# Batch 0 of a linear-attention and MLP kernel: q turned by 64x64 products, q.kv with 64 rows per product, and a new planned order

## The chip, the cores and the metric

The kernel runs on one core of one Trainium2 chip. The metric is the device time of one execution in microseconds; the time of before is the median of 3 runs. Rows of the profile use these names: PE is TensorE's matrix products, PEld its weight loads, DVE is VectorE, ACT is ScalarE, POOL is GpSimd, SP is SyncE, which issues most of the DMAs. "L789" is line 789 of the kernel.

## The reference

For 8 batches of 8 heads, with 576 rows of 64 numbers in each of q, k and v:

```
kv  = einsum('bhsd,bhse->bhde', k, v)            # 64x64 per head
out = einsum('bhsd,bhde->bhse', q, kv)           # 576x64 per head
out = out / sqrt(mean(out*out, -1) + 1e-6) * g_norm
x   = heads side by side: (8, 576, 512)
a1  = alpha1 * x + beta1
u   = x + lam * einsum('ts,bsd->btd', w_tok, a1)  # mixes the 576 rows
a2  = alpha2 * u + beta2
y   = u + lam * (max(a2 @ w_ch1, 0) @ w_ch2)      # 512 -> 2048 -> 512
```

## The kernel before, in words

The program is a list of operations, each with an engine, an assumed cost in microseconds, what it reads and what it writes. A list scheduler (`schedule`, L180) plays the engines forward with these costs and so fixes the order of each engine's queue and the PSUM banks; `synchronize` then puts in the waits. At run time every engine works its queue strictly in that fixed order. `plan` (L123) runs the scheduler several times, sets priorities from what it finds, and at last disturbs them at random with given seeds (`shake`, L164, here one seed, 15). It covers all operations that lie ahead of the first MLP products of batch 0. Wherever the model leaves PE without work before the first of those products, the scheduler puts a "warm" product of zeros (L1429, assumed 0.22 us) into PE's queue, so these are a fixed part of the program.

Per batch there are these stages:

- kv: k and v of a head multiplied into 64x64 (`kv_first`, L628, for batch 0; L691 and L701 for the others).
- q turned, so that the 64 columns of a head lie on partitions (`qt_first`, L649 and L663, for batch 0).
- q.kv (`qkv_groups`, L789 for batch 0; L782 and L401 for the others), and behind it the norm of each head: square (ACT, L819), sum (DVE, L821), root (ACT, L824), reciprocal (DVE, L827), multiplication into `xm`/`xtl` (DVE, L840), multiplication by alpha1, lam and g into `rt`/`rtt` (L844, DVE or POOL), multiplication by g (POOL, L848).
- token mixing with w_tok (`tok_first`, L972 for batch 0), an addition to x (L989), turning of the result (L1007) and a copy into `a2t` (L1016, L1017).
- MLP: `ch1` (L1056 with L401 for batch 0, L1075) into `ht`, and `ch2` (L1121), then the output.

w_tok itself is loaded (L1219, L1222) and turned once (L1260, L1278), and its row sums are made (L1301). w_ch1 comes in four chunks of 1 MB (L1340), each turned into bf16 by two copies (L1346); chunk i is needed by `ch1` groups 4i to 4i+3. All loads of this time go through SP in a fixed order.

Batch 0's attention is computed in fp32. Its first half (heads 0 to 3, called a=0) and second half (a=1) are loaded separately. In `qt_first`, one pair of heads takes 8 fp32 products: a stationary block of q of 128 rows (tokens) and 64 columns, and the 128x128 identity as the moving operand; the two heads of a pair fill the lower and the upper 64 partitions of one PSUM bank. A copy of 512 columns per pair (`act_dve`, L654) puts them into `qt32`. The last 64 tokens are turned in `tail` by PE's transpose operation (L663).

In q.kv of batch 0, one product takes 128 partitions of `qt32` (two heads, one above the other) and 128 tokens as the stationary operand, and a block-diagonal 128x128 `kv32` as the moving one: two 64x64 blocks of kv and two blocks of zeros, which a memset (L1229) writes. A group is two token blocks and four heads (4 products), the last group of a half is the 64 tokens at the end (2 products). So a half has three groups of 4, 4 and 2 products, and each has a norm of its own.

PE's records for fp32 products come in pairs: one product of L628, L649 or L789 leaves two records. A form such as "128*64 128x128 f32" means a stationary operand of 128 rows and 64 columns and a moving operand of 128 rows and 128 columns.

## Time and profile before

| | us |
|---|---|
| median of 3 runs | 368.47 (368.40 to 368.56) |
| the profiled execution, its own time | 368.05 |
| span in its trace | 366.2 |
| time around the span | 1.85 |
| first product of `ch1` of batch 0 on the chain | 38.63 after the span's start |
| L649 on the chain, both halves | 3.87 |
| L789 on the chain, all four pieces | 5.12 |
| warm products on the chain from 11.15 on | 3.88 |

The span is the time from the first to the last record of the traced execution. The chain of waits follows the last instruction back to whatever released each step; its pieces are given with start, length, engine and line, and "x32" is the number of records in the piece. The granted TensorE clock is 1.00 throughout.

### The profile page before, as it was taken

What the parts mean: (1) busy time and instruction counts of PE and PEld (TensorE: products, weight loads), DVE (VectorE), ACT (ScalarE), POOL (GpSimd) and SP (SyncE); (2) the same over time, 40 slices, a digit from 0 to 9 for tenths busy, and PEclk for the clock granted to TensorE, in tenths of its full rate; (3) what the DMA queues carried; (4) which work ended last, traced back from release to release, by engine and by line L of the source; (5) the groups of instructions that cost most, each with busy time, mean ns of one, the idle gap of its engine ahead of it and who ended that gap; (6) DMA issues with size and microseconds to landing.
All of it is one profiled execution on the core that took longest, in us unless ns stands there. A gap on an engine that the chain in (4) does not pass through costs nothing.

```text
span 366.2 us, 7069 instructions
## 1 busy us (share of the span) xinstructions
PE 360.6 (98%) x3164; PEld 205.8 (56%) x2876; DVE 198.4 (54%) x313; ACT 159.2 (43%) x268; POOL 81.7 (22%) x71
## 2 busy tenths in 40 slices
PE   7999999999999999999999999999999999999996
PEld 3787445467754554457654554457654554457644
DVE  4287699773973197735764176915933165720021
ACT  2464974237830298107650188107630186007600
POOL 4064602700450007100530006400620006200000
PEclk9999999999999999999999999999999999999999
DMA  8999999999777897439904499233404110420012
GB/s 257 319 290 319 384 382 273 265 250 249 211 141 158 246 259 178 101 94 309 230 18 115 138 304 177 50 110 85 90 7 108 59 30 0 59 100 30 0 57 88
DMA packets 92423, 59.87 MB, mean 163 GB/s; under 512 B 59549, under 2 KB 82341, under 8 KB 92264
## 3 DMA queue, kind: packets, MB, share of 16 engines
q1 hardware_dynamic: 92368, 59.41, 62.5%
q8 instruction: 24, 0.39, 0.5%
q14 instruction: 7, 0.06, 0.0%
q10 hardware_dynamic: 24, 0.01, 0.0%
HBM read 38.56 MB, written 9.44 MB: 131 GB/s over the span
## 4 chain that ended last, share of the span: by engine, by line
PE 97%; DMA 2%; SPq 0%; DVE 0%; issue 0%
PE ps L1121 34%; PE ps L1075 19%; PE ps L1056 16%; PE ps L920 8%; PE ps L691 4%; DMA qf<-in_q_dram 2%; PE ps L401 2%; PE ps L782 2%; PE ps L789 1%; PE ps L942 1%; PE ps L972 1%; PE ps L1007 1%; PE ps L1429 1%; PE ps L649 1%; PE ps L1102 1%; PE ps L701 1%
## 5 line engine op out<-in xcount | busy, mean ns | idle before, releaser
L1121 PE MATMUL ps<-w,ht 128*128 128x512 bf16 x560 | 126.0, 379 | 0.0
L848 POOL TENSOR_TENSOR xm<-xm,g_bc 128x512 f32<-128x512 f32 (+1 forms) x36 | 47.4, 1316 | 186.6 <-DVE rt L844 184.7
L1121 PEld LDWEIGHTS ps<-w,ht 128*128 128x128 bf16 x560 | 53.1, 98 | 63.0 <-issue 1.2
L1045 ACT ACTIVATE ht<-ps,hb 128x512 bf16<-128x512 f32 (+1 forms) x96 | 70.5, 739 | 40.5 <-PE ps L1075 32.8
L1075 PE MATMUL ps<-a2t,w 128*128 128x320 bf16 x512 | 71.9, 299 | 0.0
L1075 PEld LDWEIGHTS ps<-a2t,w 128*128 128x128 bf16 x512 | 49.3, 98 | 20.2 <-ACT ht L1045 0.3
L1056 PE MATMUL ps<-a2t,w 128*128 128x512 bf16 x256 | 59.7, 379 | 0.0
L1131 DVE TENSOR_TENSOR xm<-ps,xm 128x512 f32<-128x512 f32 x31 | 21.4, 689 | 50.4 <-PE ps L1121 50.3
L718 ACT ACTIVATE kvd<-ps 64x128 bf16<-64x128 f32 x28 | 7.6, 271 | 78.5 <-PE ps L701 78.1
L1056 PEld LDWEIGHTS ps<-a2t,w 128*128 128x128 bf16 x256 | 24.3, 97 | 29.6 <-issue 1.2
L821 DVE TENSOR_REDUCE small<-sq 128x16 f32<-128x1024 f32 (+2 forms) x20 | 20.5, 1028 | 22.9 <-ACT sq L819 22.9
L920 PE MATMUL ps<-rt,wt 128*128 128x512 bf16 x112 | 28.8, 379 | 0.0
L501 ACT ACTIVATE qs<-qf 128x1024 bf16<-128x1024 f32 (+1 forms) x15 | 14.2, 964 | 26.7 <-DMA qf<-in_q_dram 26.1
L927 DVE TENSOR_TENSOR xm<-ps,xm 128x1024 f32<-128x1024 f32 x14 | 17.1, 1222 | 14.5 <-PE ps L920 14.5
L1046 ACT ACTIVATE ht<-ps 128x512 bf16<-128x512 f32 (+1 forms) x32 | 20.6, 650 | 6.8 <-PE ps L1075 3.3
L819 ACT ACTIVATE sq<-ps 128x1024 f32<-128x1024 f32 (+2 forms) x20 | 17.4, 873 | 7.3 <-PE ps L789 4.3
L840 DVE TENSOR_TENSOR xm<-ps,small 128x1024 f32<-128x1024 f32 (+1 forms) x18 | 19.8, 1103 | 0.4
L723 DVE TENSOR_TENSOR kvd<-ps,kvd 64x128 bf16<-64x128 f32 x28 | 8.1, 288 | 20.5 <-ACT kvd L718 20.0
L844 DVE TENSOR_TENSOR rt<-xm,e1g_bc 128x1024 bf16<-128x1024 f32 (+1 forms) x17 | 19.0, 1125 | 0.1
L582 DVE TENSOR_TENSOR qs<-qf,qs 128x1024 bf16<-128x1024 f32 x12 | 15.3, 1284 | 6.8 <-ACT qs L501 6.8
L920 PEld LDWEIGHTS ps<-rt,wt 128*128 128x128 bf16 x112 | 10.9, 98 | 12.9 <-issue 0.4
L691 PEld LDWEIGHTS ps<-vf,kf 128*64 128x64 f32 x448 | 14.2, 138 | 5.0 <-issue 5.0
(119 smaller groups left out, 334.2 us busy)
## 6 DMA issues: line engine op xcount, KB each, us to landing
out_dram<-xm SPq DMA_DIRECT2D x31, 256.0 KB, 2.5
kf<-in_k_dram SPq DMA_DIRECT2D x7, 1024.0 KB, 10.3
vf<-in_v_dram SPq DMA_DIRECT2D x7, 1024.0 KB, 8.0
qf<-in_q_dram SPq DMA_DIRECT2D x7, 1024.0 KB, 8.0
stg<-in_moe_w_ch_dram SPq DMA_DIRECT2D x3, 1024.0 KB, 13.8
kf<-in_moe_w_ch_dram SPq DMA_DIRECT2D x2, 1024.0 KB, 14.6
kf<-in_k_dram SPq DMA_DIRECT2D x2, 576.0 KB, 5.2
vf<-in_v_dram SPq DMA_DIRECT2D x2, 576.0 KB, 6.3
```

Of the source, the lines that this page charges most:

```text
L691: m = e.matmul(out(h), kf[:, buf, h, c, :], vf[:, buf, h, c, :], start=(c == 0 and h < 4 * a + 2), stop=False, skip_group_check=True)
L821: P.op("DVE", dve_us(64 * m), lambda e: e.tensor_reduce(out=smv, in_=sqv.rearrange("p (h d) -> p h d", h=m), axis=AX.X, op=ALU.add), r=[(" ...
L840: P.op("DVE", dve_us(64 * m), lambda e: e.tensor_tensor(out=x3, in0=split(raw()), in1=inv, op=ALU.mult), r=[t, ("sm", sms)], w=xk, pri=-200)
L844: lambda e: e.tensor_tensor(out=r_, in0=x, in1=eb, op=ALU.mult),
L848: P.op("POOL", pool_us(64 * nh), lambda e, xc=xc: e.tensor_tensor(out=xc, in0=xc, in1=g_bc[rows, None, :].to_broadcast([nr, nh, DH]), op=A ...
L920: m = e.matmul(t.ap()[:, i, :], tok_w(b, sc, c), rsrc(b, sc), start=(sc == 0), stop=(sc == 4))
L1045: o = P.op("ACT", act_us(n) + 0.09, lambda e: e.activation(dst, src(), ACT.Relu, bias=hb[:, fj:fj + 1]) if b > 1 else e.activation(dst, sr ...
L1046: dst, src(), ACT.Relu, bias=hb[:, fj:fj + 1]) if b > 1 else e.activation(
L1056: m = e.matmul(t.flat(), w, a2t[:, dj, 0:512], start=(dj == 0), stop=(dj == 3))
L1075: m = e.matmul(t.ap()[:, i, 0:320], w1[:, dj, 128 * fj:128 * fj + 128], a2t[:, dj, 320 * i:320 * i + 320], start=(dj == 0), stop=(dj == 3))
L1121: m = e.matmul(t.flat(), ht[:, fj, 128 * c:128 * c + 128], w2[:, fj, :], start=(fj == 0), stop=(fj == 15))
L1131: P.op("DVE", dve_us(512), lambda e: e.tensor_tensor(out=x, in0=t.flat(), in1=x, op=ALU.add), r=[t] + keys, w=keys)
```

## The change

- `qt_first`: the two pairs of a half become one operation `main(a)` with 32 products. Each takes 64 rows (tokens) and 64 columns of one head as the stationary operand and a 64x64 corner of the identity as the moving one; the four products of a set lie in the four 64x64 quarters of the array: rows by token half `r`, output partitions by head `x`. The output goes to two banks, one for each token half, and two copies of 512 columns (two runs of 256) take it into `qt32`. The transposes of the last 64 tokens stay.
- `kv32` holds only the 64x64 blocks, one above the other; its memset goes, and the copies behind `kv_first` write columns 0 to 63.
- q.kv of batch 0: `first(hs)` replaces the three groups of a half. Its first operation has 16 products: 64 rows of `qt32` (one head) by 128 tokens as the stationary operand, 64 columns of `kv32` as the moving one. The lower head of each pair writes one bank, the upper head another, and they take turns. A second operation does the 64 tokens at the end with 4 products into two banks. Three norms follow: two of 512 columns (two heads, all four token blocks), one of 256 columns that reads two banks.
- The norm's code becomes a function of its own, `norm`, used by both kinds of groups. The keys that order readers and writers of x and rt are kept for 2 heads instead of 4. POOL's multiplication by g takes pieces of 256 columns as before in batch 0.
- The assumed costs: 1.12 for `main` (before 0.95 for each of two pairs), 1.0 and 0.2 for the two operations of `first` (before 0.28 for each token block, so 1.4 a half).
- `shake` uses other shares and widths, and the plan takes four seeds, (2, 103, 114, 147), in place of (15,).

```diff
@@ shake
-            return {o: pri[o] + (rnd.gauss(0.0, 2.0) if rnd.random() < 0.1 else 0.0)
+            share, by = (0.02, 0.1, 0.3)[seed % 3], (1.0, 3.0)[seed % 2]
+            return {o: pri[o] + (rnd.gauss(0.0, by) if rnd.random() < share else 0.0)
                     for o in movable}
@@ kv_first
-                        e, kv32[rows, 2 * a:2 * a + 2, 64 * h:64 * h + 64],
-                        t.ap(rows)[:, :, 0:64]), r=[t, "kvz"], w=[("kv32", a, h)])
+                        e, kv32[rows, 2 * a:2 * a + 2, 0:64], t.ap(rows)[:, :, 0:64]),
+                        r=[t], w=[("kv32", a, h)])
@@ qt_first
-            def pair(pr):
-                t = P.ptile(1)
+            def main(a):
+                t = P.ptile(2)
 
                 def f(e):
-                    for c in range(4):
-                        for h in range(2):
-                            m = e.matmul(t.flat(slice(64 * h, 64 * h + 64))[
-                                :, 128 * c:128 * c + 128], qf[:, 4 * (pr // 2) + 2 * h + pr % 2, c, :], ident[:],
-                                start=True, stop=True)
+                    for y in range(2):
+                        for c in range(4):
+                            for x, r in ((0, 0), (0, 1), (1, 0), (1, 1)):
+                                rows = slice(64 * r, 64 * r + 64)
+                                o = 256 * y + 64 * c
+                                m = e.matmul(t.ap(slice(64 * x, 64 * x + 64))[:, r, o:o + 64],
+                                             qf[rows, 4 * a + 2 * x + y, c, :],
+                                             ident[rows, rows], start=True, stop=True)
                     return m
-                P.op("PE", 0.95, f, r=["ident", ("qf", pr // 2)], w=[t])
-                P.op(act_dve(512), 0, lambda e: copy(e, qt32[:, pr, 0:512], t.flat()),
-                     r=[t], w=[("q32", pr)])
+                P.op("PE", 1.12, f, r=["ident", ("qf", a)], w=[t])
+                for y in range(2):
+                    P.op(act_dve(512), 0, lambda e, y=y: copy(
+                        e, qt32[:, 2 * a + y, 0:512].rearrange("p (c r s) -> p r c s", c=4, r=2),
+                        t.ap()[:, :, 256 * y:256 * y + 256].rearrange("p r (c s) -> p r c s", c=4)),
+                        r=[t], w=[("q32", 2 * a + y)])
@@ qkv_groups
+            def first(hs):
+                a = hs.start // 4
+                aa = [("kv32", a, i) for i in range(2)]
+                ts = [P.ptile(1) for i in range(2)]
+
+                def product(e, o, x, y, lo, n):
+                    r = slice(64 * x, 64 * x + 64)
+                    return e.matmul(o, qt32[r, 2 * a + y, lo:lo + n], kv32[r, 2 * a + y, 0:64],
+                                    start=True, stop=True)
+
+                def f(e):
+                    for c in range(4):
+                        for y in range(2):
+                            for x in range(2):
+                                o = 128 * c + 64 * y
+                                mm = product(e, ts[x].flat()[:, o:o + 64], x, y, 128 * c, 128)
+                    return mm
+                P.op("PE", 1.0, f, r=QT + KVD + aa + [("q32", 2 * a), ("q32", 2 * a + 1)], w=ts)
+                for x, t in enumerate(ts):
+                    h = hs.start + 2 * x
+                    norm(t, (0, 1, 2, 3), slice(h, h + 2))
+                last = P.ptile(2)
+                rows = rows_of(0, 4)
+
+                def g(e):
+                    for y in range(2):
+                        for x in range(2):
+                            mm = product(e, last.ap(rows)[:, x, 64 * y:64 * y + 64], x, y, 512, 64)
+                    return mm
+                P.op("PE", 0.2, g, r=QT + KVD + aa + [("q32t", a)], w=[last])
+                norm(last, (4,), hs)
...
-                def f32(e):
-                    a = h0 // 4
-                    for i, c in enumerate(cs):
-                        for j in range(2):
-                            mm = e.matmul(
-                                t.flat(rows)[:, 256 * i:256 * i + 256].rearrange(
-                                    "p (x y d) -> p y x d", x=2, y=2)[:, j],
-                                qt32[:, 2 * a + j, 128 * c:min(128 * c + 128, 576)],
-                                kv32[:, 2 * a + j, :].rearrange("p (x d) -> p x d", x=2),
-                                start=True, stop=True)
-                    return mm
-                if b == 0:
-                    P.op("PE", 0.28 * nc_, f32, r=QT + KVD + [("kv32", h0 // 4, i)
-                                                             for i in range(2)]
...
@@ memsets
-        P.op("DVE", 0.4, lambda e: e.memset(kv32, 0.0), w=["kvz"])
@@ plan
-        P.plan(due, 8, (15,))
+        P.plan(due, 8, (2, 103, 114, 147))
```

More of the change, by code (lines that the diff above doesn't have):

```diff
@@ L672, in qt_first @@
             for a in range(2):
-                yield lambda a=a: pair(2 * a)
-                yield lambda a=a: pair(2 * a + 1)
+                yield lambda a=a: main(a)
                 yield lambda a=a: tail(a)
@@ L754, in xkeys @@
             base = ("x", b % 2, c) if c < 4 else ("xt", (b // 2) % 2, b % 2)
-            return [base + (a,) for a in range(hs.start // 4, hs.stop // 4)]
+            return [base + (a,) for a in range(hs.start // 2, hs.stop // 2)]
         def rkeys(b, c, hs=ALL[0]):
             base = ("rt", b % 2, c) if c < 4 else ("rtt", b % 2)
-            return [base + (a,) for a in range(hs.start // 4, hs.stop // 4)]
+            return [base + (a,) for a in range(hs.start // 2, hs.stop // 2)]
         cnt = {"ch": 0}
         def qkv_groups(b):
+            def first(hs):
[26 more added lines that the diff above has]
+                norm(last, (4,), hs)
             def group(cs, hs):
@@ L768, in group @@
                 t = P.ptile((m + 7) // 8)
-                rows = rows_of(b, cs[0])
-                nr = rows.stop - rows.start
-                n = cnt["ch"]
-                cnt["ch"] += 1
-                sqs, sms = n % 2, n % 4
                 aa = range(hs.start // 4, hs.stop // 4)
@@ L784, in f, with norm @@
                     return mm
-                def f32(e):
-                    a = h0 // 4
-                    for i, c in enumerate(cs):
-                        for j in range(2):
-                            mm = e.matmul(
-                                t.flat(rows)[:, 256 * i:256 * i + 256].rearrange(
-                                    "p (x y d) -> p y x d", x=2, y=2)[:, j],
-                                qt32[:, 2 * a + j, 128 * c:min(128 * c + 128, 576)],
-                                kv32[:, 2 * a + j, :].rearrange("p (x d) -> p x d", x=2),
-                                start=True, stop=True)
-                    return mm
-                if b == 0:
-                    P.op("PE", 0.28 * nc_, f32, r=QT + KVD + [("kv32", h0 // 4, i)
-                                                             for i in range(2)]
-                         + ([("q32", h0 // 2), ("q32", h0 // 2 + 1)] if cs[0] < 4
-                            else [("q32t", h0 // 4)]), w=[t])
-                else:
-                    P.op("PE", 0.059 * m + 0.03, f,
-                         r=[("qt", c, a) for c in cs for a in aa]
-                         + [("kvd", a, h, i) for a in aa for h in range(2) for i in range(3)],
-                         w=[t])
+                P.op("PE", 0.059 * m + 0.03, f,
+                     r=[("qt", c, a) for c in cs for a in aa]
+                     + [("kvd", a, h, i) for a in aa for h in range(2) for i in range(3)],
+                     w=[t])
+                norm(t, cs, hs)
+            def norm(t, cs, hs):
+                h0, nh, nc_ = hs.start, hs.stop - hs.start, len(cs)
+                m = nc_ * nh
+                rows = rows_of(b, cs[0])
+                nr = rows.stop - rows.start
+                n = cnt["ch"]
+                cnt["ch"] += 1
+                sqs, sms = n % 2, n % 4
+                two = t.n == 2 and m <= 8
                 def raw():
+                    if two:
+                        return t.ap(rows)[:, :, 0:32 * m]
                     return t.flat(rows)[:, 0:64 * m]
                 def split(ap):
+                    if two:
+                        return ap.rearrange("p x (y d) -> p x y d", d=DH)
                     if nc_ > 1:
@@ L819, in group @@
                 P.op("ACT", act_us(64 * m), lambda e: e.activation(
-                    sqv, raw(), ACT.Square), r=[t], w=[("sq", sqs)])
+                    sqv.rearrange("p (x f) -> p x f", x=2) if two else sqv, raw(),
+                    ACT.Square), r=[t], w=[("sq", sqs)])
                 P.op("DVE", dve_us(64 * m), lambda e: e.tensor_reduce(
@@ L833, in group @@
                     eb = e1g_bc[rows, None, lo:hi].to_broadcast([nr, nc_, 64 * nh])
-                    gb = g_bc[rows, None, None, :].to_broadcast([nr, nc_, nh, DH])
                 else:
@@ L837, in group @@
                     eb = e1g_bc[rows, lo:hi]
-                    gb = g_bc[rows, None, :].to_broadcast([nr, nh, DH])
                 xk = [kk for c in cs for kk in xkeys(b, c, hs)]
+                if two:
+                    inv = smv.rearrange("p (x y) -> p x y", x=2)[:, :, :, None].to_broadcast(
+                        [nr, 2, nh // 2, DH])
                 P.op("DVE", dve_us(64 * m), lambda e: e.tensor_tensor(
-                    out=x3, in0=split(raw()), in1=inv,
+                    out=x3.rearrange("p (x y) d -> p x y d", x=2) if two else x3,
+                    in0=split(raw()), in1=inv,
                     op=ALU.mult), r=[t, ("sm", sms)], w=xk, pri=-200)
@@ L845, in group @@
                      r=xk + ["e1"], w=[kk for c in cs for kk in rkeys(b, c, hs)], pri=-100, port=True)
-                for i, c in enumerate(cs):
-                    xc = x3[:, i] if nc_ > 1 else x3
-                    P.op("POOL", pool_us(64 * nh), lambda e, xc=xc: e.tensor_tensor(
-                        out=xc, in0=xc, in1=g_bc[rows, None, :].to_broadcast([nr, nh, DH]),
-                        op=ALU.mult), r=xkeys(b, c, hs) + ["g"], w=xkeys(b, c, hs), pri=-50)
+                if nc_ < 4:
+                    parts = [((c,), x3[:, i] if nc_ > 1 else x3) for i, c in enumerate(cs)]
+                else:
+                    parts = [((i, i + 1), x3[:, i:i + 2]) for i in range(0, 4, 2)]
+                for cs_, xc in parts:
+                    k2 = [kk for c in cs_ for kk in xkeys(b, c, hs)]
+                    gb = (g_bc[rows, None, :].to_broadcast([nr, nh, DH]) if len(cs_) < 2 else
+                          g_bc[rows, None, None, :].to_broadcast([nr, 2, nh, DH]))
+                    P.op("POOL", pool_us(64 * nh * len(cs_)), lambda e, xc=xc, gb=gb: e.tensor_tensor(
+                        out=xc, in0=xc, in1=gb,
+                        op=ALU.mult), r=k2 + ["g"], w=k2, pri=-50)
             def tail():
@@ L888, in tail @@
                         in1=small[own, sms, 0:4][:, :, None].to_broadcast([64, 4, DH]),
-                        op=ALU.mult), r=[t, ("sm", sms)], w=[xk[a]], pri=-200)
+                        op=ALU.mult), r=[t, ("sm", sms)], w=xk[2 * a:2 * a + 2], pri=-200)
                 x = xv(b, (4,))
@@ L897, in tail @@
                     op=ALU.mult), r=xk + ["g"], w=xk, pri=-50, port=True)
-            for hs in (HALVES if b == 0 else ALL):
-                for cs in PAIRS:
-                    yield (lambda cs=cs, hs=hs: group(cs, hs)) if b == 0 or cs != (4,) else tail
+            if b == 0:
+                for hs in HALVES:
+                    yield lambda hs=hs: first(hs)
+                return
+            for cs in PAIRS[:2]:
+                yield lambda cs=cs: group(cs, ALL[0])
+            yield tail
         def tok_w(b, sc, c):
@@ L1001, in group @@
                                                   else xkeys(b, c))
-                        if kk[-1] == dj // 2]
+                        if kk[-1] == dj]
                 def f(e):
@@ L1106, in halves @@
                          + [("ht", n) for n in range(16)], w=[t])
-                    keys = [xkeys(b, c)[i]]
+                    keys = xkeys(b, c)[2 * i:2 * i + 2]
                     P.op("DVE", dve_us(256), lambda e, t=t, cols=cols: e.tensor_tensor(
@@ L1324, in bass_transnormer_attn__then__resmlp_affine_kernel @@
         for i in range(2):
-            for a in range(2):
+            for a in range(4):
                 P.lastw[("rtt", i, a)] = P.lastw["rtt0"] + P.lastw[("rtt1", i)]
```

## The prediction

> **What bounds the kernel now.** I read the page first, for the engine that is never free, then the chain of waits in the stretch that the diff touches.

> ```profile
> span 366.2 us, 7069 instructions
> ...
> PE 360.6 (98%) x3164; PEld 205.8 (56%) x2876; DVE 198.4 (54%) x313; ACT 159.2 (43%) x268; POOL 81.7 (22%) x71
> ...
> DMA  8999999999777897439904499233404110420012
> ...
> PE 97%; DMA 2%; SPq 0%; DVE 0%; issue 0%
> ```

> PE is busy for 98% of the span, and 97% of the chain that ended last is PE. So a microsecond taken out of PE's queue is worth up to a microsecond, if nothing else is then late. The DMA engines are full in the first quarter: a load can't be hurried by computing earlier. Batch 0's part of the chain, by start, length, engine and line:

> ```profile
> 8.76 1.97 PE ps L649 x32
> ...
> 12.52 1.67 PE ps L789 x12
> 14.19 1.21 PE ps L628 x72
> 15.40 1.09 PE ps L789 x8
> 16.49 1.90 PE ps L649 x32
> 18.39 0.27 PE ps L663 x2
> 18.65 1.62 PE ps L1429 x7
> 20.27 1.78 PE ps L789 x16
> 22.05 0.48 PE ps L1260 x4
> 22.53 0.68 PE ps L1278 x5
> ...
> 26.60 0.58 PE ps L789 x4
> ...
> 29.36 1.08 PE ps L691 x32
> ...
> 36.69 1.94 PE ps L1429 x9
> 38.63 0.21 PE ps L1056
> ```

> From 8.76, when q's first half has landed, to 38.63, when `ch1` begins, PE goes from one piece to the next without a hole. After that nothing touched by the diff runs, so the question is how much earlier `ch1` can begin. The touched pieces are L649 (1.97 + 1.90 = 3.87 us) and L789 (1.67 + 1.09 + 1.78 + 0.58 = 5.12 us). L1429 is PE's own filler, 1.62 + 1.94 us here: its count is fixed by the planner's model, not by what the chip waits for.

> **Turning q.** New are 32 products of 64 rows, 64 columns and 64 moving columns a half, on four quarters of the array in turn. The trace has this form: `kv_first`. The next rows give forms (stationary rows*columns, then the moving operand), a count, busy us and mean ns of one record; a product leaves two records.

> ```profile
> L628 PE MATMUL ps<-vf,kf 64*64 64x64 f32 x144 | 2.6, 221 | 0.0
> ...
> L691 PE MATMUL ps<-vf,kf 128*64 128x64 f32 x64 | 2.3, 225 | 0.0
> ```

> L628 needs 1.21/72 = 0.0168 us a record. The new 2 x 64 records cost 128 x 0.0168 = 2.15 us, against 3.87: **-1.72 us**. The form is the same, so I put no more than 0.2 us of doubt on it. The two copies of a half now wait for all 32 products: they can start at about 8.76 + 1.08 + 0.15 = 10.0, on ACT and DVE side by side. Before, they started here, both on ACT:

> ```profile
> 9.90 0.60 ACT L501 ACTIVATE qt<-ps 128x512 f32<-128x512 f32 x1 [1.38 <-PE ps L649]
> 10.78 0.60 ACT L501 ACTIVATE qt<-ps 128x512 f32<-128x512 f32 x1 [0.28 <-PE ps L649]
> ```

> They ended at 11.38; the new ones end at about 10.7 side by side, or at 11.2 one behind the other. No wait is added.

> **q.kv, the four token blocks.** Here I part from the plan's cost of 1.0 us a half. A half had 16 records of 128 stationary and 128 moving columns; both halves together took 5.12 less the two groups of 4 tail records (0.58 each), so 3.96 us for 32 records, 0.124 each. The new half has 32 records, each with half the rows, half the moving columns, but still 128 stationary columns. They alternate between two row halves, so 16 records a half stand in sequence in each. The question is whether 0.124 is the time of the 128 moving columns or of loading the 128 stationary ones. Two forms of w_tok's turning separate it: L1278 has 128 stationary and 64 moving columns (four of five records), and the row below, from the end of L1260, has 64 stationary and 128 moving.

> ```profile
> L1260 PE MATMUL ps<-ident,ht 128*64 128x128 f32 x4 | 0.6, 272 | 0.0
> ```

> L1278 took 0.68/5 = 0.136 us a record on the chain: halving the moving columns did not shorten it at all. The second row spaces its records by (0.6 - 0.272)/3 = 0.11 us. So for 128 fp32 stationary columns the load is the limit, and halving rows and moving columns does not touch it. If the two row halves load side by side, a half takes 16 x 0.124 = 1.98 us, both 3.97: **no change (0.0 us)**. That they do is shown by L628 against L691: the same 64 by 64 columns at 0.0168 and 1.08/32 = 0.0338 us a record; splitting the rows in two halved it. The bounds: with the moving columns as the limit, 16 x 0.0675 (two of L691's intervals, its two column halves taken as one) = 1.08 us a half, -1.8 us for both; with the loads in turn, 32 x 0.124 = 3.97 a half, +4.0 us for both. I take 0.0, nearest to L1278.

> [...]

> **The 64 tokens at the end.** Before, 4 records took 0.58 us a half. Now there are 8 of 64 by 64 columns on two row halves; by L691's 0.0338 (two tiles as well) they take 0.27. Both halves: 1.16 - 0.54 = **-0.62 us**. Bounds: 0 and -0.7.

> **The rest.** The memset of `kv32` (DVE) lies before the first load has landed: nothing. The norms have the same columns per half (512, 512 and 256), so the ACT, DVE and POOL work is the same; reading two banks in one instruction is already done by the copies behind L628. What moves is that both big norms of a half become ready together. The finer keys for x add no instruction. No DMA is added or moved past another by hand; SP's order is kept by its chain.

> **Sum on PE:** -1.72 + 0.0 - 0.62 = **-2.34 us**. Does anything else become late? First w_tok, which must have landed before L1260:

> ```profile
> 7.69 0.49 SPq L1222 DMA_DIRECT2D ht<-in_moe_w_tok_dram  x1
> ...
> ht<-in_moe_w_tok_dram SPq DMA_DIRECT2D x1, 144.0 KB, 11.6
> ```

> Its last part landed at 7.69 + 11.6 = 19.3, and L1260 began at 22.05. The saving ahead of it is 1.72, plus 0.31 of the first tail, less 0.27 for the second tail, which now comes ahead of w_tok: 1.76 us. L1260 would begin at 20.3, after 19.3. The cap at this place is 22.05 - 19.3 = 2.75, and with the 0.58 us of L789 at 26.60 gone behind it, 3.3 us in all. Second, the last norm:

> ```profile
> 30.10 0.83 DVE L844 TENSOR_TENSOR rtt<-xtl,e1g_bc 64x256 bf16<-64x256 f32 x1
> ```

> The norm's last instruction ends at 30.93 because its product stood at 26.60; now that product comes before w_tok, so this chain comes earlier by more than the sum. Third, w_ch1's second chunk, for the fifth group of `ch1`:

> ```profile
> 26.37 1.74 SPq L1340 DMA_DIRECT2D w<-in_moe_w_ch_dram  x1
> ...
> w<-in_moe_w_ch_dram SPq DMA_DIRECT2D x1, 1024.0 KB, 11.6
> ...
> 41.19 1.04 ACT L501 ACTIVATE w<-w 128x1024 bf16<-128x1024 f32 x1
> ...
> 43.81 0.24 PE ps L1056
> ```

> It landed at 26.37 + 11.6 = 37.97, its two copies (1.04 us for the one shown) can follow at once, and its first use is at 43.81: over 3.5 us to spare even with the copies in turn. So 2.34 us fits through all three.

> **The filler and the new order.** The trace can't show the new order. It would cost nothing more if the filler stays at 3.56 us. Bounds: the seven at 18.65 can go (-1.62, but the cap above then holds), or the planner, which thinks PE free earlier, fills all that was saved (+2.34). I take zero, since PE runs behind its plan on L789 before and after (5.12 us against a planned 2.8; now 4.5 by my sum against 2.4), so filler placed for waits that the chip no longer sees stays about as it was.

> **The rivals.**

> 1. Moving columns set the pace of q.kv: -1.72 - 1.8 - 0.62 = -4.15 us of PE work, cut to 3.3 by w_tok's landing: 368.05 - 3.3 = 364.75. For it: L628 and L691 run at an interval that fits 64 moving columns too. Against it: L1278.
> 2. The saved time comes back as filler or as a wait (w_tok in the planner's model, or both norms of a half queueing on DVE at once): 368.05 - 2.34 + 2.34, no change. For it: filler is written into the queue wherever the model sees none ready. Against it: the last norm starts earlier, and PE had no wait on the chip.
> 3. Slower: the loads of 128 columns into the two row halves take turns, 64 records of 0.124 us in q.kv, 7.94 against 3.96 us. Then -1.72 + 3.98 and, with the tails also in turn (16 x 0.0675 = 1.08 against 1.16), -0.08: +2.2 us, so 370.25. It decides from (3.96 + 1.72 + 0.62)/64 = 0.098 us a record: above that the kernel is slower. For it: no record of before has 128 stationary columns on two row halves. Against it: L628 against L691 at 64 columns.
> 4. The turning of q does not run on four quarters as L628 does, since its moving operand is the same identity each time: it stays at 3.87, and -0.62 is left: 367.4. Nothing in the trace speaks for it.

> **How the numbers follow.** The profiled execution took 368.05 us, of which the span is 366.2 and 1.85 lie around it. The median of the runs shown is 368.47, 0.42 above, so I add 0.42 to each. Forecast: 368.05 - 2.34 + 0.42 = 366.1, chance 0.5. Rival 1: 365.2, 0.2. Rival 2: 368.5, 0.12. Rival 3: 370.7, 0.1. Rival 4: 367.8, 0.08. The range runs from 364.2, where the cap of 3.3 is reached and 1 us of filler goes with it, to 368.8, rival 2 with its spread; it leaves out rival 3 and a little at both ends. 0.2% is 0.74 us, about what a measurement of this kernel can tell from no change. Below 367.73: the forecast, rival 1, and some of 2 and 4: 0.76. Within: 0.13. Above 369.2: 0.11.

> **What would show it.** Turning of q: two pieces of 64 records in about 1.1 us each. q.kv: 32 records in about 2.0 us, the tail 8 in about 0.27; at 1.1 us rival 1 holds, at 4 us rival 3. L1260 beginning near 20.3, `ch1` near 36.3, filler still about 3.6 us; with rival 2 the filler or holes on PE are near 6. I am wrong if `ch1` begins where it did, or if the time behind `ch1` changes by over 0.5 us, which I hold for fixed.

## The result, and the profile after

| | before | after |
|---|---|---|
| median, us | 368.48 | 371.80 |
| lowest to highest of 4 runs | 368.40 to 368.56 | 371.00 to 371.98 |
| the profiled execution's own time | 368.05 | 371.73 |
| span in its trace | 366.2 | 369.8 |
| first product of `ch1` on the chain | 38.63 | 42.18 |
| span behind that product | 327.57 | 327.62 |

The ratio is 1.0086, 95% interval 1.0068 to 1.0103. The kernel became 3.3 us slower; 366.1 was forecast. All of it arises ahead of `ch1`, in the stretch that the prediction worked through. One run below, of 377.36 us in E7 with the clock at 0.982, counts as a slow one and is left out of its ratio. The page of after:

```profile
span 369.8 us, 7290 instructions
...
PE 365.0 (99%) x3278; PEld 207.5 (56%) x2990; DVE 198.4 (54%) x317; ACT 159.0 (43%) x266; POOL 79.4 (21%) x68
...
PEclk9799999999999999999999999999999999999999
...
q8 instruction: 24, 0.39, 0.4%
...
PE 99%; DVE 0%; issue 0%
```

PE is busier than before (365.0 us against 360.6), with 114 more products and 114 more loads, and its clock dips in the second of the 40 slices. The chain of waits of after, by start, length, engine and line (L653 and L670 are the turning of q and its tail, L778 the new q.kv, L629 `kv_first`, L1472 filler, L1242 the products of one row that stood at L1198, L1303 the turning of w_tok):

```profile
9.07 1.09 PE ps L653 x64
...
11.48 1.05 PE ps L1242 x2
12.53 3.51 PE ps L778 x40
16.04 2.13 PE ps L629 x72
18.16 1.82 PE ps L1472 x4
19.98 0.39 PE ps L670 x2
20.37 0.32 PE ps L1472
20.70 1.09 PE ps L653 x64
21.79 1.19 PE ps L1472 x5
22.97 0.38 PE ps L778 x8
...
24.10 1.93 PE ps L778 x32
26.04 0.68 PE ps L1303 x4
...
41.21 0.97 PE ps L1472 x4
```

Each turning takes 1.09 us, as forecast. The second half of q.kv takes 1.93 for 32 records and 0.38 for 8. But the first half, 40 records as well, took 3.51, L629 took 2.13 where it had taken 1.21, and four filler products took 1.82. The windows of after say why. Their columns are the stretch, its length, busy us and instructions of PE, PEld, DVE, ACT and POOL, the granted clock, DMA share and GB/s:

```profile
12.00:13.00 1.00, 1.00 (x13) 0.47 (x12) 0.00 (x0) 0.43 (x1) 0.00 (x0) 1.00 1.22 290
13.00:14.00 1.00, 1.00 (x16) 1.00 (x16) 0.00 (x0) 0.16 (x1) 0.00 (x0) 0.70 1.10 319
14.00:15.00 1.00, 1.00 (x14) 1.00 (x12) 0.00 (x0) 0.00 (x0) 0.00 (x0) 0.50 0.87 350
...
19.00:20.00 1.00, 1.00 (x4) 0.17 (x3) 0.00 (x0) 0.68 (x3) 0.00 (x0) 0.50 1.13 351
20.00:21.00 1.00, 1.00 (x27) 0.67 (x31) 0.59 (x3) 0.00 (x0) 0.00 (x0) 0.89 1.17 245
```

From about 13.4 to 20.2 us PE ran at half clock (0.50), without a moment of idleness ahead of it (busy for 11.40 of 11.40 us from 2.00 to 13.40). The 3.55 us at `ch1` then come out of the chain like this:

| piece of the chain | before | after | difference | forecast |
|---|---|---|---|---|
| turning of q | 3.87 | 2.18 | -1.69 | -1.72 |
| q.kv with its tails | 5.12 | 5.82 | +0.70 | -0.62 |
| `kv_first`, second half | 1.21 | 2.13 | +0.92 | 0 |
| filler from 10.9 us on | 3.88 (17) | 6.88 (25) | +3.00 | 0 |
| all else | | | +0.62 | 0 |

"All else" is mostly a later begin (+0.31) and one small product of L1242 (0.36) that now stands behind q's landing. The number of filler products stands in brackets. About 3.1 us of the table are the half clock: 3.51 - 2.31 in q.kv (2.31 is its length at full clock in E2 below), 0.92 in L629, 0.90 in the four filler products, 0.13 in L670. Eight more filler products at 0.22 are 1.8 us. On this reading alone the clock would be the culprit. The experiments speak against that.

### The profile page after: what moved, and what is told of

Its sections match the earlier page's. It is cut to its first block, busy times and chain, and to the rows that moved or that the text cites. A ratio compares the mean times of both kernels' runs of the same rounds, so it can differ in the third digit from the quotient of the medians.

```text
span 369.8 us, 7290 instructions
## 1 busy us (share of the span) xinstructions
PE 365.0 (99%) x3278; PEld 207.5 (56%) x2990; DVE 198.4 (54%) x317; ACT 159.0 (43%) x266; POOL 79.4 (21%) x68
## 4 chain that ended last, share of the span: by engine, by line
PE 99%; DVE 0%; issue 0%
PE ps L1165 33%; PE ps L1119 19%; PE ps L1100 15%; PE ps L964 8%; PE ps L697 4%; PE ps L1472 4%; PE ps L402 2%; PE ps L815 2%; PE ps L778 2%; PE ps L986 1%; PE ps L1016 1%; PE ps L1051 1%; PE ps L1146 1%; PE ps L629 1%; PE ps L707 1%; PE ps L1303 1%
## 5 line engine op out<-in xcount | busy, mean ns | idle before, releaser
L1119 PEld LDWEIGHTS ps<-a2t,w 128*128 128x128 bf16 x512 | 49.3, 98 | 20.2 <-ACT ht L1089 0.3
L853 DVE TENSOR_REDUCE small<-sq 128x16 f32<-128x1024 f32 (+2 forms) x20 | 20.3, 1026 | 24.6 <-ACT sq L850 24.6
L583 DVE TENSOR_TENSOR qs<-qf,qs 128x1024 bf16<-128x1024 f32 (+1 forms) x14 | 18.0, 1286 | 7.7 <-ACT qs L502 7.6
L1090 ACT ACTIVATE ht<-ps 128x512 bf16<-128x512 f32 (+1 forms) x32 | 20.1, 649 | 4.0 <-PE ps L1119 2.5
## 6 DMA issues: line engine op xcount, KB each, us to landing
kf<-in_k_dram SPq DMA_DIRECT2D x7, 1024.0 KB, 10.8
vf<-in_v_dram SPq DMA_DIRECT2D x7, 1024.0 KB, 9.4
qf<-in_q_dram SPq DMA_DIRECT2D x7, 1024.0 KB, 8.6
stg<-in_moe_w_ch_dram SPq DMA_DIRECT2D x3, 1024.0 KB, 14.7
kf<-in_moe_w_ch_dram SPq DMA_DIRECT2D x2, 1024.0 KB, 13.6
```

The source lines that it names most:

```text
L853: P.op("DVE", dve_us(64 * m), lambda e: e.tensor_reduce(out=smv, in_=sqv.rearrange("p (h d) -> p h d", h=m), axis=AX.X, op=ALU.add), r=[(" ...
L1090: dst, src(), ACT.Relu, bias=hb[:, fj:fj + 1]) if b > 1 else e.activation(
L1119: m = e.matmul(t.ap()[:, i, 0:320], w1[:, dj, 128 * fj:128 * fj + 128], a2t[:, dj, 320 * i:320 * i + 320], start=(dj == 0), stop=(dj == 3))
```

## The experiments

"E1" and so on are the kernels in the order in which they ran. All ratios are against the kernel before, run beside them; its median was 368.26 to 368.58. Short code cuts show each edit, some of them shortened.

**E1, the old operations in the new plan.** The rival: the seeds made the order bad.

```
kernel before, with the new shake() and
-        P.plan(due, 8, (15,))
+        P.plan(due, 8, (2, 103, 114, 147))
```

> The kernel before with the new shake and the four seeds (2, 103, 114, 147), nothing else. Main theory (the loss is filler that the planner puts where its model sees PE free, plus a half clock that the new 64-row products of q.kv bring on): the queue holds 18 filler products after the first turning of q against 17 in the kernel before, so 368.5 plus 0.2, full clock throughout. Rival (the new seeds are simply a worse order): slower by 1 us or more, 369.5 to 371.5.

369.21, ratio 1.0026 [1.0016, 1.0036], clock 1.00. That lies between the theory's 368.7 and the rival's 369.5: with the old operations the new order costs 0.9 us. With the new operations it doesn't add to the loss, as E2 shows.

**E2, the new operations in the old plan.**

```
kernel after, with the old shake() and
-        P.plan(due, 8, (2, 103, 114, 147))
+        P.plan(due, 8, (15,))
```

> The changed kernel with the old shake and seed 15. Main theory: 26 filler products after the first turning of q, against 25 in the changed kernel and 17 in the kernel before, and the half clock again between about 13 and 20 us: 371.5 to 372.5. Rival (the seeds): the forecast of 2.3 us of saved PE work comes through, 366 to 367.

372.51, ratio 1.0128 [1.0100, 1.0156]: not better, so the seeds aren't the cause. The profiled run took 371.95 with the clock at 1.00, where half clock was expected (the other three had 0.990 to 0.995), so half clock isn't needed for the loss either. Its page and chain (L652 turning, L777 q.kv, L1471 filler):

```profile
PEclk9999999999999999999999999999999999999999
```

```profile
12.37 2.31 PE ps L777 x40
...
17.44 1.09 PE ps L652 x64
18.53 0.16 issue
18.69 0.38 PE ps L1471
19.07 2.04 issue
21.11 0.81 PE ps L1471 x3
21.92 0.38 PE ps L777 x8
...
41.45 0.22 PE ps L1099
```

PE stands still from 19.07 to 21.11 and nothing releases it ("issue"), and this before a filler product of zeros, which needs no data. Such a stop is called a hole below. One row of the page has played no part so far: the queue of instructions, 24 packets and 0.39 MB, so 16 KB each. One of them starts in the window from 18.50 to 18.75:

```profile
q8 instruction: 1, 0.02, 28.8%
```

The holes in the runs below are 0.85 to 2.75 us long (and 0.24 in E12).

The packets follow PE. In all sixteen traces the first packet starts 1.9 to 3.8 us after PE has passed record 193, that is 256 ahead of 449, and the second one 3.1 to 4.7 us after record 449; E13, where more work for PE lies early, passes 193 at 6.04 us in place of 9.04 and has its first packet at 9.08 in place of 11.34. The traces also have 24 packets for 6070 to 6344 records of PE, and 25 in E13 and E14, with 6516 and more.

**E3 and E4, one part alone,** each in the old plan.

```
E3: kernel before with qt_first() of after (cost 1.12)
E4: kernel before with kv32, first() and norm() of after (costs 1.0 and 0.2)
```

> The kernel before with q turned by 64x64 products alone; q.kv, shake and seed as before. Main theory: full clock, since q.kv is the old one with 128 rows; PE work falls by 1.7 us, but the queue holds 31 filler products against 17, 14 x 0.23 = 3.2 us, so 368.5 - 1.7 + 3.2 = 370.0. Rival A (filler stands in for waits that would be there anyway, and only the clock costs time): 367 to 368. Rival B (the turning by 64x64 products brings on the half clock): half clock in this run, 371 or more.

370.59, ratio 1.0063 [1.0044, 1.0083], clock 0.999 to 1.00. The turning is short (1.09 us a half), but 28 filler products stand behind the first one, against 17, and `ch1` begins at 40.40. That fits the filler's part of the theory, but E11 below shows that the last 13 of these products stand mostly where PE would have waited anyway.

> The kernel before with the new q.kv (64 rows per product) alone; turning of q, shake and seed as before. Main theory: the 64-row products bring on the half clock near 13 to 20 us; filler is 17 products as before, so 368.5 - 0.3 (PE work) + 2 to 3 (half clock) = 370 to 371.5. Rival (the clock has another cause, such as the shorter turning ahead of the low-activity products): full clock, 368.0 to 368.6.

370.52, ratio 1.0065 [1.0050, 1.0080], clock 0.999. Full clock was the rival's condition, so the theory's cause is refuted: the 64-row products of q.kv alone don't lower the clock. `ch1` begins at 38.76, only 0.13 later; the loss lies behind it. From 75 to 90 us PE is busy 12.60 us (15.00 before):

```profile
75.00:90.00 15.00, 12.60 (x109) 8.02 (x94) 10.15 (x18) 5.88 (x12) 1.89 (x1) 1.00 1.08 246
```

In the chain PE waits there for DVE's copies, and DVE stands still without a releaser for 1.64 and 0.99 us. So the time came out as expected by luck, for another reason. Whether DVE's own instructions were late is only argued.

**E5 and E6, short filler,** to take away the filler's time but not its instructions.

```
after (E5) and before (E6): filler of model time above 9.0
-            return e.matmul(t.flat(), wz[:, 0:128], wz, start=True, stop=True)
+            n = 512 if full else 16
+            return e.matmul(t.flat()[:, 0:n], wz[:, 0:128], wz[:, 0:n], start=True, stop=True)
```

> The changed kernel with its queue order unchanged, but every filler product that the planner's clock puts after 9 us has 16 moving columns in place of 512, so that it takes next to no time. Main theory (the filler is fixed in the queue behind a PE that is already late, and most of it stands for no wait on the chip): of the 6.9 us of filler after the first turning about 4 go, the rest comes back as waits: 368 to 369.5 if the clock holds as it did, more if less filler makes the half clock longer. Rival (the filler covers waits that are there on the chip): 371 to 372.

372.28, ratio 1.0102 [1.0078, 1.0125]: a miss. With the filler's time gone PE came to the border earlier and stood still from 18.86 to 21.46, 2.60 us. The clock was at half from 14.5 to 17.9, and again from 21.3, where the hole was about to end, to 31.5.

> The kernel before with the same edit: filler products after 9 us have 16 columns. 3.9 us of filler can go; the last nine cover the wait for the copies into a2t, the seven ahead of q.kv's second half only in part. Main theory: 367 to 368 at full clock; the difference between this and the same edit of the changed kernel is what the new operations themselves are worth, and the theory says that it is under 1 us. Rival (the filler costs nothing): 368.3.

367.23, ratio 0.9969 [0.9959, 0.9980], `ch1` at 37.92: as expected. In the old kernel, which comes to the border late and has no hole there, shorter filler is a gain of 1.0 us.

**E7, more filler early,** to keep the clock up.

```
after, ahead of the 512-column product of L1242
+                    for i in range(4 if n > 64 else 0):
+                        P.warm[1](e, P.warm[3])
```

> The changed kernel with four filler products of 512 columns added just ahead of the 512-column product of one row (alpha1 lam g), that is in the stretch from 10 to 13.4 us after which the clock fell by half. Main theory (that stretch, with transposes, products of one row and then 64-row products, holds too little work, and the clock falls at its end): the clock stays at 1.00, the four products cost 0.9 us and the 3 us of half clock are saved: 369.5 to 370.3. Rival (the 64-row products themselves bring the clock down whatever stands before): clock 0.99 again and 372.5.

372.23, ratio 1.0105 [1.0085, 1.0125]: a miss. The clock fell for one short stretch in the profile (15.2 to 18.6) and in one other run not at all, and that run took 371.72. In the profile a hole stands within the second turning:

```profile
19.87 1.08 PE ps L653 x62
20.96 0.85 issue
21.81 0.27 PE ps L653 x2
```

The border fell two records short of the end of the turning: 62 of its 64 records, and 695 instructions in the count.

**E8, the measured costs,** so that the planner doesn't think PE free.

```
after
-  main tail 0.14, first 1.0 and 0.2, small row product 0.2, seeds (2, 103, 114, 147)
+  main tail 0.27, first 1.95 and 0.38, small row product 0.36, seeds (3, 140, 210, 380)
```

> The changed kernel planned with the costs that the trace shows: 1.95 and 0.38 us for the two operations of q.kv (in place of 1.0 and 0.2), 0.27 for the turning of the last tokens (0.14), 0.36 for the small product of one row (0.2), and seeds (3, 140, 210, 380). The planner's own start of ch1 goes from 35.9 to 38.7, 2.0 us of it by the costs. Main theory (the chip's PE was late against a plan with costs half as long, and fixed filler kept it late): ch1 starts within 1.5 us of the plan, at 39 to 40.2, and the time is 368.4 to 369.6. Rival (costs in the plan do not matter, the new operations are slow themselves): 371 to 372.

373.59, ratio 1.0142 [1.0127, 1.0157]: a miss. PE stood still at about 694 again, from 18.84 to 21.31, and ran at half clock from 22.3 to 32.6.

**E9, the old operations with more instructions.** The decisive one: nothing of the change is in it. Every product of L649 is cut into two of 64 columns, and the first 13 filler products into one load and eight products of 64 columns.

```
kernel before
+  for z in range(2): matmul(..., ident[:, 64 * z:64 * z + 64])
+  early filler: 1 load, 8 products of 64 columns
```

> The kernel before, order unchanged, with more and smaller instructions on PE ahead of 18.7 us and nearly the same work: each product of L649 is cut into two of 64 moving columns (+64 records of loads and products a half, about +0.2 us a half) and each of the first 13 fillers into 8 of 64 columns with one weight load (+91). By 18.65 us PE then has had about 725 loads and products instead of 506; in all runs of the new operations that reached the place at full clock PE stood still after 694 of them, until 21.1 to 21.8 us. Theory (PE runs out of fetched instructions there): a hole of 1.5 to 2.5 us with no releaser ends at about 21.3; 369.5 to 371. Rival (the hole belongs to the new products, their banks or their waits): no hole, 368.5 to 368.9.

371.35, ratio 1.0089 [1.0069, 1.0110], about the changed kernel's own loss (1.0086). The clock stayed at 1.00 in the profile:

```profile
16.53 1.72 PE ps L651 x51
18.24 2.13 issue
20.37 0.68 PE ps L651 x13
...
41.30 0.22 PE ps L1058
```

The hole is in the middle of a turning whose data has landed, at about 695 instructions. `ch1` begins 2.67 us later than in before: 2.13 are the hole, and the cut turnings take 0.59 more in themselves (4.46 against 3.87). The hole's packet starts in the window from 17.50 to 17.75 and the hole ends 2.7 us later:

```profile
q8 instruction: 1, 0.02, 29.7%
```

**E10, half of batch 1's k and v not loaded.** The rival to "asked for late": the packet is slow because the DMA queues are full.

```
E8, batch 1's main k and v loads (heads 0 to 3 stay unloaded, their result is not the reference's)
+                hs = slice(4, 8) if b == 1 else slice(0, 8)
```

> The kernel planned with the measured costs (the one that showed a hole from 18.84 to 21.31 us), with batch 1's main loads of k and v cut to heads 4 to 7, so that 1 MB less stands in the queues from 8 to 22 us; batch 1's output lacks the right k and v of four heads. Theory (the 16 KB packet of instructions stands behind the loads): the packet begins before 18.7 and the hole ends at 20.3 or earlier. Rival (the fetch is asked for late and takes a fixed time): the hole ends at 21.0 to 21.6 as before.

372.77 (one run). The hole is no shorter:

```profile
17.85 1.09 PE ps L654 x64
18.94 2.75 issue
21.69 0.59 PE ps L1473 x2
```

1 MB less brought the packet's start from 18.81 in E8 to 18.66, and the end of the hole no earlier (21.69 against 21.31).

**E11, E3 with the short filler of E5.**

```
E3, and the edit of E5 (filler of 16 columns)
```

> The kernel with the turning of q alone, filler after 9 us with 16 columns. Theory (the turning is worth its 1.7 us once filler does not eat it; it puts 64 more loads and products a half in PE's queue, but with the old q.kv PE comes to number 694 only after 21.3 us): ch1 near 37, 366.3 to 367.2, against 367.2 of the kernel before with the same filler. Rival (a wait of another engine or the clock takes it): 367.5 to 369.

370.55, ratio 1.0067 [1.0043, 1.0091]: a miss, no faster than E3. There are two holes now, 1.07 us at 14.91 (about 441 instructions) and 1.12 us at 21.95 (about 694). And toward the end the chain leaves PE for DVE's addition to x and for ACT's copies into `a2t`:

```profile
36.66 1.21 DVE xm L994 x2
...
39.01 1.44 ACT a2t L1021 x2
...
40.50 0.39 PE ps L1061
```

PE is idle there for 1.04 and 1.36 us, 2.40 in all, where E3 had 13 filler products, 2.96 us, and `ch1` begins at 40.50 against 40.40 in E3. So most of that part of E3's filler stood for waits which are there without it.

**E12, the turning alone, planned anew.** If work that needs few instructions lies ahead of the border, the turning should pay.

```
E11 with costs 0.55 a token block for the old q.kv (0.28), 0.27 and 0.36 as in E8
-        P.plan(due, 8, (15,))
+        P.plan(due, 8, (0, 9, 13, 16, 42, 180, 186, 338))
```

> The turning of q alone with the old q.kv, planned with the costs that the trace shows (0.55 for each token block of q.kv in place of 0.28, 0.27 for the turning of the last tokens, 0.36 for the small product of one row), seeds (0, 9, 13, 16, 42, 180, 186, 338), and 16-column filler after 9 us. The planner's start of ch1 is 36.58 with costs that are true, against 35.84 with costs that were too short in the kernel before. Theory: ch1 at 37 to 37.8, 366.3 to 367.3, faster than the kernel before and than its small-filler version. Rival (without filler the clock falls): 369 or more.

366.45, ratio 0.9940 [0.9924, 0.9957], as expected, and faster than both kernels. The profiled run had half clock from 12.3 to 15.7, the five others 1.00. E12 differs from before by the turning, the short filler, the costs and the seeds at once. The short filler alone gave the old kernel 367.23 (E6); the old turning with these costs and seeds was not run. The border is now reached within the turning of w_tok (L1265), at 22.92, where the packet had started in the window from 20.00 to 20.25, and PE stands still for 0.24 us:

```profile
22.00 0.92 PE ps L1265 x6
22.92 0.24 issue
23.16 1.42 PE ps L1265 x10
...
37.53 0.38 PE ps L1061
```

**E13 and E14, 180 instructions more ahead of q,** in E2 and in after: the first 12 filler products are cut into one load and 16 products of 32 columns. If the count sets the place, the border moves.

```
+            e.matmul(t.flat()[:, 0:32], wz[:, 0:128], wz[:, 0:32], start=True, stop=True)
+            for i in range(1, 16):
+                m = P.matmul_held(t.flat()[:, 32 * i:32 * i + 32], wz[:, 0:128],
+                                  wz[:, 32 * i:32 * i + 32], True, True)
```

> The changed operations under the old plan (the run whose profile had full clock and a hole of 2.04 us ending at 21.11), with the first 12 fillers each cut into 16 products of 32 columns behind one weight load: 180 more instructions before 6.5 us, nothing else. Theory (PE's instructions come in blocks of about 256, the next block lands about 6 us after PE enters the last one it has, and the block borders stand at 440 and 694 loads and products): the border that held PE at 694 now stands 180 earlier in the work, is met near 15.5 us, and its block lands near 16.2; PE passes the second turning of q without a hole of over 0.8 us, comes to w_tok 1 to 2 us earlier, and more instructions make the kernel faster: 370 to 371 against 371.9. Rival (the supply is not it; the turning or the wait behind it is): the hole stays at the same product near 19 to 21 us, 372 or more.

376.82, ratio 1.0212 [1.0174, 1.0251]. The time was missed, the place was not: the border at about 444 moved into the first turning.

```profile
9.06 0.91 PE ps L652 x43
9.97 1.65 issue
11.62 0.77 PE ps L652 x21
```

I had left out that this earlier border makes a hole too, and that half clock follows: 11.8 to 25.5 us, with q.kv's first half at 4.23 us. The second border made no hole any more.

> The changed kernel itself with the same edit. Theory: at full clock the hole that its half clock hid does not come back, so 370 to 370.8; where the clock falls by half in one or two windows it is up to 1 us more, 371 to 371.8. The rest above the kernel before is filler (25 products against 17 after the first turning) and stays. Rival (the half clock alone made it slower): unchanged at 371.8 when the clock is 0.991, and back at 368.5 to 369 when it is 1.00.

376.95, ratio 1.0211 [1.0171, 1.0252]: the same miss, with a hole of 1.98 us at 9.94, behind 43 records of the first turning. So it doesn't tell what after would do at full clock.

## Why the prediction was wrong

The measured 371.8 lies above every number that was given; the highest was rival 3's 370.7.

- **The turning, -1.72 us:** right, -1.69 in after, and 1.09 to 1.16 us a half wherever it stands whole on the chain at full clock (0.93 in one half of E12).
- **q.kv without a change, 0.0 us:** right at full clock, 1.93 us a half against 1.98. Rival 1 (1.1 us a half) and rival 3 (4.0) are both refuted. The tails came to 0.38 each, so -0.40 in place of -0.62.
- **The rest late?** Right for w_tok, the norms and w_ch1: no wait for them stands on the chain of after. The time behind `ch1` changed by 0.05 us, as held; but it isn't fixed in general, since it rose by 0.9 us in E2 and 2.4 in E4. Rival 4 fell with the turning.
- **The step that failed: "The filler and the new order ... I take zero".** The chain holds 3.00 us more of filler. I argued that the planner's filler would stay about as it was, since PE runs behind its plan. But the planner lays its filler by its own costs, not by the chip's: its `ch1` starts at 35.84 in its own schedule of before and at 35.9 in that of after, so nearly all that the new costs saved went back into the queue as 8 products of zeros, 1.8 us. That is rival 2's mechanism, the bound of +2.34 that I gave and did not take. How much of the 1.8 us is lost is not shown by itself: in E3 and E11 a good part of the filler stands for waits, and E5, after with short filler, ran into a hole.
- **The step that was missing: PE's own instructions.** "Does anything else become late?" looked at three transfers and not at the fetch of the program. The change doubles the instructions of the turning and of q.kv. In before, PE reaches instruction 694 at about 29.7 us, and the packet behind it starts at 20.1. In E2, E5 and E8, new operations that meet the border without after's long half clock, it gets there at 18.8 to 19.1 us, while the packet starts at 18.5 to 18.8 and the hole ends at 21.1 to 21.5. So in these runs what was saved ahead of this border was not kept; E9 has such a hole with the old operations (2.13 us), and E13 at a border that was moved (1.65 us).
- **The clock.** It was 1.00 throughout before, and I took that for granted. In after half clock takes 3.1 us, by the table. But because of it PE gets to the border only at about 22.2 us, about when the packet (its start is in the window from 19.50 to 19.75) can have landed (the holes end 2.4 to 3.0 us after it), and no hole is left. E2's profiled run and one run of E7, at clock 1.00, were no faster. So the two don't add up: with the new operations the work behind the border started at 21.1 to 21.8 us in E2, E5, E7, E8 and E10, by the hole, and at 22.2 in after, by the half clock. For after itself this is inferred, since its own trace has no hole and E14 did not settle it.

In E2 the account up to `ch1` is: turning -1.62, q.kv -0.50, the two stops at 18.53 and 19.07 +2.20, filler 5.73 (21 products) against 3.88, +1.85; the rest, +0.9, is in small pieces, the largest the small product of L1241 (0.36) and three more short stops (0.37 together). Thus the 2.1 us that the operations save are lost once to the hole, and the filler is longer by nearly as much again.

**What stays open.** What brings the half clock on at 13.4 us in after. No idle time of PE lies ahead of that stretch of 6.8 us, so idleness alone doesn't explain it. In E5, E8, E10, E13 and E14 half clock came behind holes of 1.65 to 2.75 us, in E2 and E9 a hole of 2.04 and 2.13 was followed by none. The place of the hole seems to matter. In each trace the changes of the clock ahead of `ch1` lie whole multiples of 3.41 us apart (after: 6.57, 13.40, 20.22; E5: 4.23, 14.47, 17.89, 21.30, 31.54). Cut into such steps, the five holes with half clock behind them fill 1.59 (E10) to 2.44 us (E5) of the step that ends where it begins, and the others at most 1.58 of one (E2). These two lie too near each other for a rule, and nothing was run to test it. Open too: what sets the time from a border to the next packet's start (E10 says only that 1 MB less of other traffic hardly hastens it), and E4's loss behind `ch1`. The trace does not name the engine that a packet is for; that these are PE's rests on their times and on the counts.

## What to carry to other kernels

Cutting a product into smaller ones can be right in its own time and still lose: count the instructions that PE issues in a stretch, and where 256 of them pass within the 6 us or so that a packet took here (in E2 PE passed the first border at about 14.9 us and got past the second at 21.11; from border to border it was 5.6 to 7.2 us wherever there was a hole), look for a hole that nothing releases. Filler that a planner lays by assumed costs can take back what a faster operation saves, so look at the new chain before judging the operation, and shorten the filler to see which of it stands for waits. Measured costs alone didn't help here (E8). E12 is one way out: the faster turning, with instruction-poor work ahead of the border and little filler, was 2.1 us faster than before. Of these, 1.0 is what the short filler gave alone in E6; the turning's own share is not shown.

## What the runs showed of the hardware

- PE stood still for 0.85 to 2.75 us at about 441 or about 694 of its loads and products in nine of the fourteen kernels, with the border in turnings, filler, `kv_first` or q.kv. The hole ended 2.4 to 3.0 us after the packet of 16 KB had started.
- Loads of 128 columns into two row halves run side by side: 1.93/32 = 0.060 us a record, half of the 0.124 of the full-height ones.
- A hole of 2 us or more can go with 10 us of half clock (E5, 21.3 to 31.5) or with none (E9); the time of such a kernel spreads more between runs than that of before (E11: 369.98 to 373.04 with clocks of 1.00 to 0.986; before in the first comparison: 368.40 to 368.56).
